# A transformer block on one core: each engine's order of work given as a list, with other bank limits and another start

## The chip, the cores and the metric

The kernel runs on one core of one Trainium2 chip. Five queues of the core appear in the trace: PE (matrix products), ACT, DVE and POOL (work on tiles, element by element), and SP, which here does nothing but start DMA transfers. PEld is PE's loading of the operand that stays in place. The metric is the time of one execution on the device, in microseconds (us). A time is the median of three runs unless the text says otherwise. Where the trace is read, the numbers are those of one profiled execution.

## The reference

One block on x of 2048 rows by 512 columns, float32, with adaptive layer norm, memory-augmented attention (32 heads of 16 columns, four segments of 512 rows) and a feed-forward part of 1792 columns.

```python
mod = (_silu(c) @ w_mod).reshape(c.shape[0], 6, 1, -1)
sa, ca, ga, sb, cb, gb = (mod[:, 0], mod[:, 1], mod[:, 2], mod[:, 3], mod[:, 4], mod[:, 5])
h = _layernorm(x, axis=-1) * (1 + ca) + sa
x = x + ga * _A_ref(h, A_wq, A_wk, A_wv, A_wo, A_beta)
h = _layernorm(x, axis=-1) * (1 + cb) + sb
x = x + gb * _B_ref(h, B_w1, B_b1, B_w2, B_b2)
...
    # inside _A_ref, for each of the four segments s
    logits = jnp.einsum("bhqd,bhkd->bhqk", qs, ks) * scale + mask
    p = _softmax(logits, axis=-1)
    a_dot = jnp.einsum("bhqk,bhkd->bhqd", p, vs)
    num = jnp.einsum("bhld,bhde->bhle", pq, M)
    den = jnp.einsum("bhld,bhd->bhl", pq, z)[..., None] + 1e-6
    o = g * (num / den) + (1.0 - g) * a_dot
    M = M + jnp.einsum("bhld,bhle->bhde", pk, vs)
    z = z + jnp.einsum("bhld->bhd", pk)
...
    # inside _B_ref
    r = jnp.where(h > zero, h, zero)
    out = jnp.einsum("bsf,fd->bsd", r * r, w2) + b2
```

## The kernel before, in words

Most matrix products are made from operands split into a high part and a rest (`hi`, `lo`), three products for one, so every weight and every activation that enters them is first split by a cast on ACT and a subtraction on DVE or POOL.

The attention is cut into 16 units `u` (four segments times four groups of eight heads), each unit into two quads of four heads, 32 quads in all. For a unit, `qk` projects queries and keys (tiles `bqk`, lines L536 to L538), ACT and DVE split them into `sg`, and twelve DMAs on SP spread `sg` into `ST`. For a quad, `a_quad` makes scores only to find each row's maximum (tiles `ba`, L617; ACT copies some to `ac`, DVE reduces the rest at L622). The maxima are transposed on PE (`bat`, L678), negated on ACT (`mt`, L680) and put into a row of `ST` by two small DMAs on SP (L685). `b_quad` then makes the scores again with the maximum inside (`bpb`, L759), ACT takes the exponential into `pt` (L774), POOL clears the masked part, and PE multiplies with the values (`bpv`, L816). ACT copies the result out, PE turns it (`bfin`, L842) and DVE normalises it. `vproj` makes the values (`bv`), `mem` the memory part (`bpkt`, `bmu`, `bmr`). Behind the attention stand the output projection (`bwot`, `bwop`, L900 to L902), the second layer norm (`blnq`, L413, fed by `xh` from DVE, L409) and the feed-forward part (`bh`, `bpf`). At the start, `mod_cols` computes the scale and shift of the first layer norm (`bmod`, L365, then `bmodc`, L385), `split_w` splits wq, wk and wv by four column groups (L476, L479), `ln1` makes `HT`, the transposed input of all projections, and small products of the identity (`bwarm`, L334) fill PE while it has nothing else.

PE runs in three shapes of its array, which the planner calls modes: `F`, the whole array (`bqk`, `bv`, `bwop`, `bh`, `bpf` and the transposes); `R`, two halves of 63 or 64 rows side by side (`ba`, `bpb`); `C`, four groups of 32 columns (`bpv`, `bmod`).

Nothing is left to a scheduler of the language: class `Plan` runs over all steps (`op`), each with an engine, an assumed duration, a due number `pr` and what it needs, and fixes the order of every engine before the program is written. Among the steps that are ready, an engine takes the one with the smallest due number; PE's choice (`pick_pe`) may stay in its mode a little longer (`STAY`), gather an amount (`BATCH`) or wait (`PATIENCE`). PSUM has eight banks, and `POOLS` limits how many each kind may hold: 4 for `#A` (`ba`), 3 for `#B` (`bpb`), 1 for `#V` (`bpv`), 3 for `#D` (most others). Engines keep the order so found, whatever then happens on the chip.

Of the kernel before, what the change touches and what calls it, by code (L numbers as in the profile page):

```python
# [13 lines left out]
ALU = mybir.AluOpType  # L14
# [19 lines left out]

N_WARM = 60
BATCH = {"R": 0, "C": 1.28, "F": 0.28}
K_A = (0.08, 1.18)
K_B = (1.46, 2.6)
K_F = 3.4
K_FF = 3.98  # L40
K_L2 = 0.37
K_LN = (-2.92, -1.85)
# [12 lines left out]
PATIENCE = 1.22  # L55
STAY = {"R": 0.53, "C": 0, "F": 0.38}
# [6 lines left out]
class Plan:  # L63
# [52 lines left out]
    def pick_pe(self, ready):  # L116
        best, amount = {}, {}
        for n in ready:
            if self.can(n):
                if n.mode not in best or (n.pr, n.seq) < (best[n.mode].pr, best[n.mode].seq):  # L120
                    best[n.mode] = n
                amount[n.mode] = amount.get(n.mode, 0.0) + n.dur
        if not best:
            return None
        first = min(best.values(), key=lambda n: (n.pr, n.seq))
        cur = best.get(self.mode)
        if cur is not None and cur.pr <= first.pr + self.stay[self.mode]:
            return cur
        if first.mode == self.mode:
            return first  # L130
        if amount[first.mode] < self.batch[first.mode]:

            rest = [n for m, n in best.items() if m != first.mode and
                    (m == self.mode or amount[m] >= self.batch[m]) and n.pr <= first.pr + self.patience]
            if rest:
                return min(rest, key=lambda n: (n.mode != self.mode, n.pr, n.seq))
        return first

    def run(self):
# [3 lines left out]
        free = dict.fromkeys(engs, 0.0)  # L143
        self.mode = "F"
# [4 lines left out]
        ev, k, t, wire, out = [], 0, 0.0, 0.0, []  # L149
        todo = len(self.nodes)  # L150
        while todo:
            moved = True
            while moved:
                moved = False
                for e in engs:
                    if free[e] > t:
                        continue
                    if e == "PE":
                        n = self.pick_pe(ready[e])
                    else:  # L160
                        n = min((x for x in ready[e] if self.can(x)), key=lambda x: (x.pr, x.seq), default=None)
# [5 lines left out]
                    if e == "PE" and n.mode != self.mode:  # L167
                        s = max(t, free[e] + 0.1) + self.LDW[n.mode]
# [4 lines left out]
                    end = s + n.dur  # L173
                    if n.nb:
# [32 lines left out]
def block_kernel(ctx, tc, x, wq, wk, wv, wo, beta, w1, b1, w2, b2, c, wmod, out):  # L207
# [96 lines left out]
    nc.scalar.dma_start(cs, c[0].rearrange("(k p) -> p k", p=P))  # L304
# [19 lines left out]
    n1 = op("NIL", 4.2, lambda: None, PR0)  # L324
    n1 = op("ACT", 0.2, lambda: nc.scalar.activation(cneg, cs, AF.Exp, scale=-1.0), PR0, after=[n1])
# [818 lines left out]
```

## Time and profile before

| what | value |
|---|---|
| time, median of 3 runs | 841.67 us (841.42 to 841.98) |
| time of the profiled execution | 843.69 us |
| its span, first to last instruction | 842.0 us |
| mean granted clock of TensorE | 0.990 |
| busy time of POOL | 211.5 us (25%) |

The times outside the table stand in the prediction, with their rows. A row of the stretches gives the stretch in us from the span's start, its length, the busy time of each engine with its number of instructions, the granted clock (1.00 is full), the share of time in which the 16 DMA engines moved data, and GB/s. A row of the timeline gives the start, how long it took, engine, line, operation, output and inputs, shape and count, and in brackets the idle time ahead of it with what ended it. Products on PE overlap, so the distance from one start to the next says what a product costs, and its duration does not.

### The profile page before, as it was taken

The page shows a single profiled execution, that of the slowest core. Times are in us where ns is not written, and L with a number is a line of the kernel's source. Part 1 is how long each engine was busy: PE and PEld are TensorE (multiplying, and loading weights), DVE is VectorE, ACT ScalarE, POOL GpSimd, SP SyncE. Part 2 cuts the span into 40 slices and gives each one's busy share as a digit, 9 for nine tenths or more (in the row PEclk, how much of TensorE's full clock was granted, in tenths as well). Part 3 has the DMA queues.
Part 4 walks back from the last instruction along what each step waited for, and adds up shares of the span by engine and source line. Part 5 has one row for each costly group of instructions (what it writes and reads, how often), then busy time and mean ns, then how long its engine had stood idle before and what let it go on. Part 6 is the DMA issues. An engine that isn't in the chain of part 4 may idle for free.

```text
span 842.0 us, 14276 instructions
## 1 busy us (share of the span) xinstructions
PE 819.5 (97%) x4956; PEld 592.8 (70%) x4956; DVE 549.6 (65%) x1503; ACT 441.0 (52%) x907; POOL 211.5 (25%) x262
## 2 busy tenths in 40 slices
PE   9899999999999999999999979999999999999998
PEld 8675666766656666666556657888888888888886
DVE  4678877887887888578879768977534334323223
ACT  2637965678856789567764444454333223322211
POOL 2614542456635666334412110000000000000000
PEclk9899999999999999999999998999999999999999
DMA  8634454232432234322252304233100010001001
GB/s 293 167 90 105 126 172 131 72 77 72 111 77 68 71 76 117 77 66 66 65 150 98 97 18 141 85 100 88 63 1 1 0 51 1 1 0 51 1 0 51
DMA packets 50377, 65.19 MB, mean 77 GB/s; under 512 B 8449, under 2 KB 22529, under 8 KB 50306
## 3 DMA queue, kind: packets, MB, share of 16 engines
q1 hardware_dynamic: 49634, 64.14, 27.2%
q8 instruction: 40, 0.66, 0.3%
q14 instruction: 31, 0.25, 0.1%
q10 hardware_dynamic: 672, 0.13, 0.1%
HBM read 29.91 MB, written 7.34 MB: 44 GB/s over the span
## 4 chain that ended last, share of the span: by engine, by line
PE 85%; DVE 7%; ACT 4%; DMA 2%; issue 1%; SPq 0%; DVEq 0%; ACTq 0%
PE bpv L816 8%; PE bpb L759 7%; PE bh L1065 6%; PE bh L1064 6%; PE bh L1066 6%; PE bpf L1092 6%; PE bpf L1094 6%; PE bpf L1093 6%; PE ba L617 5%; PE bqk L536 4%; PE bqk L537 3%; PE bqk L538 3%; PE bwop L900 2%; PE bv L588 2%; DVE ba L622 2%; PE bwop L902 2%
## 5 line engine op out<-in xcount | busy, mean ns | idle before, releaser
L622 DVE CUSTOM_DVE_ANT_0 ba<-ba,msk 128x512 f32<-128x512 f32 (+2 forms) x384 | 191.8, 533 | 38.2 <-PE ba L617 33.3
L774 ACT ACTIVATE pt<-bpb 128x512 f32<-128x512 f32 x320 | 176.9, 617 | 51.2 <-PE bpb L759 49.2
L1074 ACT ACTIVATE r<-bh,b1c 128x512 f32<-128x512 f32 x56 | 38.5, 688 | 180.4 <-PE bh L1066 163.3
L763 POOL TENSOR_SCALAR_AFFINE_SELECT pt<-pt 128x512 f32<-128x512 f32 x128 | 81.0, 645 | 182.5 <-ACT pt L774 181.0
L1081 DVE TENSOR_TENSOR r<-r 128x512 f32<-128x512 f32 x56 | 38.7, 691 | 126.8 <-ACT rr L1078 126.7
L759 PE MATMUL bpb<-ST 64*128 64x256 f32 (+2 forms) x512 | 87.1, 387 | 1.7 <-DVE X1L L859 1.2
L1092 PE MATMUL bpf<-W,rr 128*128 128x512 f32 x224 | 88.1, 393 | 0.0
L1094 PE MATMUL bpf<-W,rr 128*128 128x512 f32 x224 | 88.0, 393 | 0.0
L1093 PE MATMUL bpf<-W,rr 128*128 128x512 f32 x224 | 88.0, 393 | 0.0
L816 PE MATMUL bpv<-pt,VT 128*32 128x512 f32 (+3 forms) x1024 | 85.2, 443 | 0.9 <-ACT pt L774 0.9
L759 PEld LDWEIGHTS bpb<-ST 64*128 64x128 f32 x512 | 43.3, 184 | 48.4 <-issue 17.0
L617 PE MATMUL ba<-ST 63*128 63x256 f32 (+2 forms) x512 | 72.3, 336 | 1.4 <-ACT lnf L419 0.5
L536 PE MATMUL bqk<-HT,WQK 128*128 128x512 f32 x128 | 58.0, 453 | 3.8 <-ACT HT L426 3.8
L617 PEld LDWEIGHTS ba<-ST 63*128 63x128 f32 x512 | 50.0, 186 | 11.9 <-DVE mx L622 2.2
L816 PEld LDWEIGHTS bpv<-pt,VT 128*32 128x32 f32 x1024 | 26.2, 109 | 41.5 <-issue 35.0
L622 DVE DVE_READ_ACCUMULATOR2_ANT mx<- 128x1 f32 x384 | 54.4, 142 | 0.0
L537 PE MATMUL bqk<-HT,WQK 128*128 128x512 f32 x128 | 51.3, 401 | 0.0
L538 PE MATMUL bqk<-HT,WQK 128*128 128x512 f32 x128 | 51.3, 400 | 0.0
L1092 PEld LDWEIGHTS bpf<-W,rr 128*128 128x128 f32 x224 | 42.1, 188 | 10.0
L1093 PEld LDWEIGHTS bpf<-W,rr 128*128 128x128 f32 x224 | 42.0, 188 | 9.8
L1094 PEld LDWEIGHTS bpf<-W,rr 128*128 128x128 f32 x224 | 42.0, 188 | 9.8
L1064 PE MATMUL bh<-H2a,W 128*128 128x512 f32 x112 | 45.1, 403 | 0.0
(161 smaller groups left out, 1597.4 us busy)
## 6 DMA issues: line engine op xcount, KB each, us to landing
ST<-sg SPq DMA_DIRECT2D x192, 128.0 KB
wr<-in_B_w SPq DMA_DIRECT2D x28, 256.0 KB
xt<-in_A_x SPq DMA_DIRECT2D x16, 256.0 KB
wm<-in_w_mod SPq DMA_DIRECT2D x16, 256.0 KB
xw<-in_A_x SPq DMA_DIRECT2D x16, 256.0 KB
o_dram<-on SPq DMA_DIRECT2D x12, 256.0 KB
ot<-o_dram SPq DMA_DIRECT2D x12, 256.0 KB
out<-X SPq DMA_DIRECT2D x12, 256.0 KB
```

The lines of the kernel that those rows point to most:

```text
L536: nc.tensor.matmul(p, wh, HT[:, 0, k], start=(k == 0), stop=False)
L537: nc.tensor.matmul(p, wh, HT[:, 1, k], start=False, stop=False)
L617: nc.tensor.matmul(dst[:, c0:c0 + n], ST[b:b + 63, 0, sl, qt * P:(qt + 1) * P], ST[b:b + 63, 1, sl, :n], start=True, stop=True)
L622: nc.vector.tensor_tensor_reduce(i, i, msk[:, 512 - n:], scale=1.0, scalar=-3e38, op0=ALU.add, op1=ALU.max, accum_out=o)
L759: nc.tensor.matmul(dst, ST[b:b + 64, 1, sl, kb * P:(kb + 1) * P], ST[b:b + 64, 0, sl, q0:512], start=True, stop=True)
L763: nc.gpsimd.affine_select(out=ap, in_=ap, pattern=[[0, ap.shape[1]], [1, P]], compare_op=ALU.is_ge, fill=0.0, base=0, channel_multiplier=-1)
L774: ns = [act(512, lambda j=j: nc.scalar.activation(buf("P", pt)[:, i + j], bank(keys[j]), AF.Exp, scale=0.25), pr[slot] + 0.01 + 0.001 * j, ...
L816: nc.tensor.matmul(bank(o)[32 * hq:32 * hq + 32, q0:q0 + src.shape[1]], v[:, a:a + 32], src, start=start, stop=stop, tile_position=(0, 32 ...
L1064: nc.tensor.matmul(p, wh, h2[:, 0, k], start=(k == 0), stop=False)
L1092: nc.tensor.matmul(p, rh, FF["W2"][:, f, 0], start=(f == 0), stop=False)
L1093: nc.tensor.matmul(p, rh, FF["W2"][:, f, 1], start=False, stop=False)
L1094: nc.tensor.matmul(p, rl, FF["W2"][:, f, 0], start=False, stop=(f == NF - 1))
```

## The change

The rule by which PE and the other engines chose is gone (`pick_pe`, `STAY`, `BATCH`, `PATIENCE`). In its place stands `ORDER`, a list of step numbers for each of PE, ACT, DVE, POOL and SP, found by a local search over the plan; `Plan.run` hands out steps in the order of the list, and when the next of the list can't start, that engine's turn waits. The assumed durations were set anew, with prices for a change of mode (`TURN`) and for a pause of PE (`PAUSE`, `COLD`).

```diff
-N_WARM = 60
-BATCH = {"R": 0, "C": 1.28, "F": 0.28}
...
+N_WARM = 70
+BANKS = {"#A": 6, "#B": 6, "#V": 1, "#D": 3}
...
-PATIENCE = 1.22
-STAY = {"R": 0.53, "C": 0, "F": 0.38}
+ORDER = {
+    "PE": """
+8 34 61 36 21 37 41 16 12 70 29 39 26 31 74 13 17 75 50 69 30 19 72 59 28 3 15 65 53 32 51 60 40 54 11 83 88 85 90
...
-    LDW = {"R": 0.11, "C": 0.03, "F": 0.11}
+    PAUSE, COLD = 1.3, 5.0
+    TURN = {"RF": 0.19, "FR": 0.17, "RC": 0.09, "CR": 0.09, "CF": 0.19, "FC": 0.15}
...
-                    if e == "PE":
-                        n = self.pick_pe(ready[e])
+                    given = self.given.get(e, ())
+                    if turn[e] < len(given):
+                        n = self.nodes[given[turn[e]]]
+                        n = n if n in ready[e] and self.can(n) else None
+                        turn[e] += n is not None
...
-    nc.scalar.dma_start(cs, c[0].rearrange("(k p) -> p k", p=P))
+    cc2 = sb.tile([KD, 2, P], F32, name="crow", tag="e0")
+    crow, cneg = cc2[:, 0], cc2[:, 1]
+    PL.held["crow"] = [("e", PL.pools["e"].pop(0))]
+    nc.scalar.dma_start(crow, c[0].rearrange("(k p) -> k p", p=P))
...
+    n1 = pe("F", 0.11, lambda: nc.tensor.transpose(bank(("cs",))[:, :KD], crow, ident[:KD, :KD]), PR0 - 1, after=[n1],
+            get=[("#D", ("cs",))], put=["crow"])
+    n_cs = op("ACT", 0.1, lambda: nc.scalar.copy(cs, bank(("cs",))[:, :KD]), PR0 - 1, after=[n1], put=[("cs",)])
...
-            h = act(512, lambda hi=hi, c0=c0: nc.scalar.copy(hi, raw()[:, :, c0]), p, sbuf=True, after=[n], put=put)
+            h = act(512, lambda hi=hi, c0=c0: nc.scalar.copy(hi, raw()[:, :, c0]), p, sbuf=True, after=[n, *(HTN[0] if cc else [])], put=put)
```

The last two pieces are the start: the vector c now comes in as four rows and is turned by PE, and the splits of all but the first column group of wq, wk and wv wait until `HT` of the first segment is done (`HTN[0]`). Ten more `bwarm` products were added. The work itself is the same.

First place, PE from the start of the program to the first projection. Before (`bwarm` are the fillers, `bmod` and `bmodc` the two modulations, `blnq` the transposes of the first layer norm):

```order
L334 MATMUL bwarm<-ident 128x128 x44
L365 MATMUL bmod<-wmod,cs 32x512 x4
L413 MATMUL blnq<-ident,xt 128x128 x8
L385 MATMUL bmodc<-selc,t 128x1 x4
L413 MATMUL blnq<-ident,xt 128x128 x8
L365 MATMUL bmod<-wmod,cs 32x512 x4
L334 MATMUL bwarm<-ident 128x128 x4
L385 MATMUL bmodc<-selc,t 128x1 x4
L334 MATMUL bwarm<-ident 128x128 x12
L536 MATMUL bqk<-HT,WQK 128x512
```

The same stretch of PE now, with the turning of c as `bcs`:

```order
L490 MATMUL bwarm<-ident 128x128 x25
L480 MATMUL bcs<-ident,crow 128x4
L490 MATMUL bwarm<-ident 128x128 x9
L521 MATMUL bmod<-wmod,cs 32x512 x8
L541 MATMUL bmodc<-selc,t 128x1 x8
L569 MATMUL blnq<-ident,xt 128x128 x8
L490 MATMUL bwarm<-ident 128x128 x2
L569 MATMUL blnq<-ident,xt 128x128 x4
L490 MATMUL bwarm<-ident 128x128 x2
L569 MATMUL blnq<-ident,xt 128x128 x4
L490 MATMUL bwarm<-ident 128x128 x19
L694 MATMUL bqk<-HT,WQK 128x512
```

Both modulations now stand together behind 34 fillers; before, the first stood behind 44, and the second behind these, sixteen transposes and the first `bmodc`. Now 57 fillers stand ahead of the first projection (60 before), and the other 13 stand among the first projections.

On ACT the same stretch held, before, from the copies of the two modulations on:

```order
L369 COPY t<-bmod 128x512 x2
L476 CAST WQK<-X1L 128x4x128 x4
L419 ACTIVATE lnf<-blnq,modc 128x128 x2
L426 CAST HT<-lnf 128x4x128
L419 ACTIVATE lnf<-blnq,modc 128x128 x2
```

and now

```order
L525 COPY t<-bmod 128x512 x2
L656 CAST WQK<-X1L 128x4x128
L575 ACTIVATE lnf<-blnq,modc 128x128 x4
L582 CAST HT<-lnf 128x4x128 x2
L575 ACTIVATE lnf<-blnq,modc 128x128 x4
```

Three of the four casts of wq have moved behind the making of `HT`, and with them their subtractions on POOL.

Second place, PE in the middle of the attention. Before, at 128 to 132 us of the span:

```order
L759 MATMUL bpb<-ST 128x512 x2
L816 MATMUL bpv<-pt,VT_106 32x256 x4
L365 MATMUL bmod<-wm,cs 32x512 x4
L759 MATMUL bpb<-ST 128x256 x2
L759 MATMUL bpb<-ST 128x384 x2
L617 MATMUL ba_1650<-ST 128x512
L617 MATMUL ba_1651<-ST 128x512
L617 MATMUL ba_1657<-ST 128x256
L617 MATMUL ba_1657<-ST 128x384
L617 MATMUL ba_1658<-ST 128x256
L617 MATMUL ba_1658<-ST 128x384
L842 MATMUL bfin<-ident,oraw 128x128 x4
```

and now, around the same values (`VT_106`):

```order
L984 MATMUL bpv<-pt,VT_106 32x384 x4
L984 MATMUL bpv<-pt,VT_106 32x128 x4
L984 MATMUL bpv<-pt,VT_106 32x256 x4
L775 MATMUL ba_1792<-ST 128x256
L775 MATMUL ba_1792<-ST 128x384
L775 MATMUL ba_1793<-ST 128x256
L775 MATMUL ba_1793<-ST 128x384
L925 MATMUL bpb<-ST 128x256 x2
L925 MATMUL bpb<-ST 128x384 x2
L925 MATMUL bpb<-ST 128x256 x2
L925 MATMUL bpb<-ST 128x384 x2
L1012 MATMUL bfin<-ident,oraw 128x128 x4
```

The pieces of `bpv` of a quad stand together more often, and so do `ba` and `bpb`. Counted over the whole of PE's order, neighbours of different modes go from 355 to 242: R to F from 103 to 68, F to R from 100 to 60, C to R from 66 to 55, C to F from 10 to 2, R to C from 63 to 47, F to C from 13 to 10.

Third place, PE at the end of the attention. Before (`blnq` is now the second layer norm's transpose, of the first segment):

```order
L816 MATMUL bpv<-pt,VT_107 32x256 x4
L413 MATMUL blnq<-ident,xh 128x128 x4
L842 MATMUL bfin<-ident,oraw 128x128 x4
L413 MATMUL blnq<-ident,xh 128x128 x8
L925 MATMUL bwot<-ident,X1L 128x128 x8
L900 MATMUL bwop<-WVO,oT 128x512
```

and now

```order
L569 MATMUL blnq<-ident,xh 128x128 x4
L984 MATMUL bpv<-pt,VT_107 32x512 x4
L984 MATMUL bpv<-pt,VT_107 32x384 x4
L984 MATMUL bpv<-pt,VT_107 32x128 x4
L984 MATMUL bpv<-pt,VT_107 32x256 x4
L1012 MATMUL bfin<-ident,oraw 128x128 x4
L1097 MATMUL bwot<-ident,X1L 128x128 x12
L1070 MATMUL bwop<-WVO,oT 128x512
```

The last transposes of the second layer norm have moved from behind the last `bpv` to ahead of it, so `bwot`, the turning of the last segment's attention result, now follows the last `bfin` at once. Behind these rows the products `bwop` of the last row tiles stand mixed with one another, and then with the first `bh`.

More of the change, by code (lines that the diff above doesn't have):

```diff
@@ L59, with numbers @@
+2095 2097 1812 2101-2102 2100 2105 2104 1832 2103 2002 1760 2218 2217 2221 2220 2222 2219 2022 2223 2228 2227 2226
[4 rows of a table added]
+""",
+}
+def numbers(text):
+    for word in text.split():
+        a, _, b = word.partition("-")
+        yield from range(int(a), int(b or a) + 1)
 class Node:
@@ L75, in __init__ @@
         self.held = {}
-        self.stay = stay
-        self.batch = batch
-        self.patience = patience
+        self.given = {e: list(numbers(text)) for e, text in order.items()}
     def op(self, eng, dur, fn, pr, after=(), mode=None, get=(), put=(), nb=0):
@@ L114, in drop @@
                     self.pools[pool].append(i)
[L116 to L137, printed above, removed]
     def run(self):
@@ L142, in run @@
         ready = {e: [] for e in engs}
-        free = dict.fromkeys(engs, 0.0)
-        self.mode = "F"
+        free = {"PE": 2.0, "ACT": 2.6, "DVE": 2.7, "POOL": 6.0, "SP": 0.8, "NIL": 0.0}
+        self.mode, turn = "F", dict.fromkeys(engs, 0)
         self.switches = 0
@@ L148, in run @@
                 ready[n.eng].append(n)
-        ev, k, t, wire, out = [], 0, 0.0, 0.0, []
-        todo = len(self.nodes)
+        ev, k, t, wire, out = [], 0, 0.0, 2.6, []
+        for e in engs:
+            k -= 1
+            heapq.heappush(ev, (free[e], k, None, 0))
+        k, todo, idle, cold = 0, len(self.nodes), 0.0, 0.0
         while todo:
@@ L167, in run @@
                     if e == "PE" and n.mode != self.mode:
-                        s = max(t, free[e] + 0.1) + self.LDW[n.mode]
+                        s = t + self.TURN[self.mode + n.mode]
                         self.mode = n.mode
@@ L173, in run @@
                     end = s + n.dur
+                    if e == "PE":
+                        if s - idle > self.PAUSE:
+                            cold = s + self.COLD
+                        end += max(0.0, min(n.dur, (cold - s) / 2))
+                        idle = end
                     if n.nb:
@@ L184, in run @@
             if not ev:
-                raise RuntimeError("stuck: " + str([(n.eng, n.pr, n.get) for e in engs for n in ready[e]][:12]))
+                raise RuntimeError("the plan is stuck")
             t = ev[0][0]
@@ L647, in a_quad @@
         ac = ("ac", u, qd)
-        first = pe("R", 0.34, lambda: m1([bank(k) for k in keys]), pr[0], after=[d for pp in (2 * qd, 2 * qd + 1) for d in STN[u][pp]],
+        first = pe("R", 0.24, lambda: m1([bank(k) for k in keys]), pr[0], after=[d for pp in (2 * qd, 2 * qd + 1) for d in STN[u][pp]],
                    get=[("#A", k) for k in keys] + [("mx", mx), ("ac", ac)])
@@ L835, in b_quad @@
                    put=[("pt", u, qd, n)])
+            if n == 0:
+                turns("V", k)
         VUSE[u].append(k)
@@ L863, in b_quad @@
             if s > 0:
-                k = op("DVE" if last else "POOL", 0.6 if last else 1.45,
+                k = op("DVE" if last else "POOL", 0.6 if last else 1.24,
                        lambda: (nc.vector if last else nc.gpsimd).tensor_tensor(onv(), onv(), TL["am", u], op=ALU.add),
@@ L904, in block_kernel @@
     X1N = {}
-    WOL = []
+    WOL, XWN = [], []
     FF = {}
@@ L945, in ln2 @@
     def ln2(s, pr, wait=()):
-        r = op("DVE", 2.2, lambda: ln_rstd(st_all[:, 4 * s:4 * s + 4], 4), pr[0] - 0.1, after=[X1N[4 * s + t] for t in range(4)])
+        r = op("DVE", 2.2, lambda: ln_rstd(st_all[:, 4 * s:4 * s + 4], 4), pr[0] - 0.1, after=[X1N[4 * s + t] for t in range(4)] + (XWN if s else []))
         H2N[s] = []
```

327 lines of the change are left out of this document (241 added, 86 removed), and 4 rows, old and new, of the table ORDER.

## The prediction

> **What bounds the kernel now.** I read the page first, for its shares of busy time and its chain.
>
> ```profile
> PE 819.5 (97%) x4956; PEld 592.8 (70%) x4956; DVE 549.6 (65%) x1503; ACT 441.0 (52%) x907; POOL 211.5 (25%) x262
> ...
> PE 85%; DVE 7%; ACT 4%; DMA 2%; issue 1%; SPq 0%; DVEq 0%; ACTq 0%
> ```
>
> PE is busy for 97% of the span, and 85% of the chain that ended last is PE's own. So the time can only fall where PE idles, where its clock is low, or where its busy time holds less than it could. Second I read the stretches, cut where the program's stages change.
>
> ```profile
> 0.00:23.20 23.20, 21.22 (x168) 19.09 (x168) 11.35 (x38) 6.45 (x13) 8.04 (x20) 1.00 0.90 283
> 23.20:27.00 3.80, 0.03 (x1) 0.00 (x0) 3.37 (x5) 3.71 (x10) 0.98 (x1) 0.88 1.04 194
> 27.00:33.00 6.00, 5.97 (x14) 4.41 (x15) 3.42 (x6) 4.52 (x10) 3.97 (x4) 0.51 0.82 277
> 33.00:60.00 27.00, 27.00 (x133) 20.53 (x132) 17.78 (x54) 9.91 (x30) 10.46 (x9) 1.00 0.36 85
> 60.00:420.00 360.00, 356.09 (x2673) 228.66 (x2672) 286.47 (x940) 263.15 (x580) 173.13 (x208) 1.00 0.35 91
> 420.00:433.00 13.00, 10.22 (x67) 5.92 (x66) 11.33 (x36) 9.38 (x18) 3.12 (x5) 0.87 0.71 204
> 433.00:496.00 63.00, 62.48 (x421) 41.98 (x420) 48.11 (x132) 30.02 (x60) 11.83 (x18) 1.00 0.25 80
> 496.00:511.00 15.00, 9.43 (x48) 6.91 (x48) 13.18 (x38) 7.87 (x16) 0.00 (x0) 0.77 0.33 104
> 511.00:838.00 327.00, 327.00 (x1440) 265.26 (x1439) 153.67 (x257) 106.00 (x175) 0.00 (x0) 1.00 0.11 33
> 838.00:842.00 4.00, 0.10 (x1) 0.00 (x0) 0.89 (x3) 0.00 (x0) 0.00 (x0) 0.98 0.64 228
> ```
>
> The first busy column is PE's. Three places lose time openly: the start (3.8 us idle, then 6 us at a clock of 0.51), 420 to 433 us (2.8 us idle, clock 0.87) and 496 to 511 us (5.6 us idle, clock 0.77). From 60 to 420 PE idles 3.9 us of 360, and from 511 to 838 not at all; the last 4 us are the final addition and store, which nothing in the change touches. In the feed-forward stretch PE has one mode and one kind of product, so no order can shorten it. What is left is PE's busy time from 33 to 496, and there I read the timeline for what a change of mode costs.
>
> ```profile
> 118.63 0.50 PE L536 MATMUL bqk<-HT,WQK 128*128 128x512 f32 x1
> 118.96 0.39 PE L537 MATMUL bqk<-HT,WQK 128*128 128x512 f32 x1
> 119.19 0.39 PE L538 MATMUL bqk<-HT,WQK 128*128 128x512 f32 x1
> ...
> 120.22 1.06 PE L816 MATMUL bpv<-pt,VT 128*32 128x512 f32 x8
> 121.10 1.04 PE L365 MATMUL bmod<-wm,cs 128*32 128x512 f32 x8
> 122.07 0.50 PE L759 MATMUL bpb<-ST 64*128 64x256 f32 x4
> 122.41 0.39 PE L617 MATMUL ba<-ST 63*128 63x512 f32 x2
> 122.73 0.50 PE L536 MATMUL bqk<-HT,WQK 128*128 128x512 f32 x1
> ...
> 414.78 0.39 PE L537 MATMUL bqk<-HT,WQK 128*128 128x512 f32 x1
> 415.00 0.39 PE L538 MATMUL bqk<-HT,WQK 128*128 128x512 f32 x1
> 415.32 0.50 PE L759 MATMUL bpb<-ST 64*128 64x256 f32 x4
> ```
>
> A `bqk` among its like takes 0.22 to 0.23 us from start to start (118.96 to 119.19, 414.78 to 415.00). The last one ahead of a change takes 0.32 (415.00 to 415.32), and the first one behind a change takes 0.33 (118.63 to 118.96). So a change costs 0.10 on the way out and 0.10 on the way in. It is the same for the others: `ba`, half the array at 512 columns, takes 0.32 ahead of `bqk` (122.41 to 122.73); the four `bpb` of 256 columns, two passes of half a `bqk`, take 0.34 instead of 0.23 behind a change (122.07 to 122.41); `bmod` takes 0.97 ahead of `bpb`, where the like `bpv` ahead of it in the same mode took 0.88. That `bpv` itself had just come in from `bqk`, so the way into C is nearly free. None of this shows as idle time; 355 changes at up to 0.20 are some 65 us inside PE's busy 819.5.
>
> **The change part by part.** *The order of PE.* The counts stand above: 94 changes fewer into F or R, at 0.20 each 18.8 us, and 19 fewer into C, at 0.10 each 1.9 us. Not every kind of group shows its way in here, so I take 20 of these 20.7 us. The bounds are 11 (113 changes, the way out alone) and 23 (113 at 0.20). All of it is on the path, since PE idles so little between 60 and 420.
>
> *The start.*
>
> ```profile
> 1.98 11.81 PE L334 MATMUL bwarm<-ident 128*128 128x128 f32 x88 [1.98 <-POOL ident masks.py:199]
> ...
> 17.48 1.06 PE L365 MATMUL bmod<-wmod,cs 128*32 128x512 f32 x8
> ...
> 19.23 2.18 ACT L476 CAST WQK<-X1L 128x512 fp32r<-128x512 f32 x4
> ...
> 20.45 3.73 POOL L479 TENSOR_TENSOR WQK<-X1L,WQK 128x512 fp32r<-128x512 f32 x3 [14.46 <-DMA ST<-pad]
> ...
> 27.03 0.79 PE L536 MATMUL bqk<-HT,WQK 128*128 128x512 f32 x1 [3.81 <-ACT HT L426]
> ```
>
> A filler is two records, so one takes 11.81 / 44 = 0.27 us. The second `bmod` starts at 17.48, and from there it is 9.55 us to the first projection, through ACT, which had four casts of wq in that way; three move behind, 1.6 us. Both `bmod` now stand behind 34 fillers, 9.1 us after 1.98. Their weights are the second and third MB that SP fetches, and at the 283 GB/s of the first stretch these 3.1 MB are there at 11 to 12 us. So `HT` could be ready at 12 + 8 = 20. But PE's own queue ahead of the projection, 57 fillers (15.3) and the `bmod`, `bmodc` and `blnq` after 1.98 (21.22 busy in the first stretch less 60 fillers is 5.1), lasts to 22.4; I take 23. That is 4.0 earlier, and with no pause ahead of it the clock stays full, where 27 to 33 lost 2.9. Of these 6.9 the 13 fillers among the projections take back 3.5. I take 3, with 0 and 7 as bounds (7 if all 13 fall into waits). The moved splits are covered by those fillers and the first 24 projections, 5.5 us: POOL takes 1.25 us for each of six, and if it is late, the projections of unit 1 wait about that long. The turning of c (one product, one copy) lies under the 34 fillers, and DVE's three short steps for it now go ahead of the layer norm's statistics. The added `bcs` costs nothing while the fillers last.
>
> *420 to 433 us.*
>
> ```profile
> 423.77 1.06 PE L816 MATMUL bpv<-pt,VT 128*32 128x512 f32 x8 [0.65 <-ACT pt L774]
> ...
> 426.57 0.51 PE L759 MATMUL bpb<-ST 64*128 64x256 f32 x4 [1.25 <-DVE X1L L859]
> ```
>
> Here output projections, modulation of the last segment and attention meet, and DVE is busy 11.33 of 13. The list sets other work between. At stake are 2.8 us of idle time and up to 0.13 x 13 = 1.7 us of clock; I take 3, with bounds 0 and 4.5. The clock fell at these pauses, the longest 1.25 us. [...]
>
> *The end of the attention.*
>
> ```profile
> 500.51 0.66 PE L842 MATMUL bfin<-ident,oraw 128*128 128x128 f32 x4
> 502.97 0.63 PE L413 MATMUL blnq<-ident,xh 128*128 128x128 f32 x4 [1.80 <-DVE xh L409]
> 506.32 1.12 PE L413 MATMUL blnq<-ident,xh 128*128 128x128 f32 x4 [2.72 <-DVE xh L409]
> ...
> 502.74 0.25 DVE L856 RECIPROCAL dn<-bfin 128x16 f32<-128x16 f32 x1
> ...
> 505.12 0.68 DVE L865 TENSOR_TENSOR X1L<-X1L,am 128x512 f32<-128x512 f32 x1
> ```
>
> The `blnq` that waited 4.5 us for DVE now stand ahead of the last `bpv`. With the lower clock (0.23 of the 9.43 us busy: 2.2) 7.8 us are at stake. But the `bwot` that follow the last `bfin` at once need that quad normalised and added: 0.9 us from L856 through L859 and 0.68 for L865, so about 2 us with the handovers, and ahead of `bfin` the copy on ACT, about 1 more. This chain was hidden behind the waiting `blnq`; it is what is late next. Another us goes to the splits ahead of `bwop`. I take 7.8 - 4 = 4, with bounds 0 and 8.
>
> *The wait that each list adds.* An engine whose next step isn't ready now holds everything behind it; on PE that is all products. The order of before was as fixed, and idled 3.9 us in 360. The new one packs the same DVE work (286.47 us there) into some 17 us less, 84% instead of 80%, so pauses must grow. Below zero the term can't go by more than those 3.9. Above, 0.65 us, the wait of the `bpv` at 423.77, once in each of the 32 quads (one `mt` each, L680 below) is 21. I take 5, that is 9 us of idle time instead of 3.9, nearer to the row of 360 us than to that of 13. The other limits of banks cost nothing by themselves: there are eight as before.
>
> The sum against the span of 842.0: -20 - 3 - 3 - 4 + 5 = -25, so 817.0. Around the span lie 843.69 - 842.0 = 1.7 us, and the profiled execution is 2.0 above the median of the runs; the forecast for the median is 817.0 + 1.7 - 2.0 = **816.7 us**.
>
> **The rivals.** *Emptying becomes the bound* (15%). PE saves its changes and waits for ACT and DVE instead, at the 21 us of the upper bound: 816.7 + 16 = 833 at worst, 828 in the middle. For it speaks 420 to 433, where DVE at 87% went with 2.8 us of pauses in 13; against it 433 to 496, with 0.5 us in 63 at 76%. [...]
>
> *The clock* (5%). If pauses like that at 426.57 come in eight more places, each can bring the 1.7 us of clock of that stretch on top of the idle time already counted: 8 x 1.7 = 13.6, so 830.
>
> *SP's queue, slower* (5%).
>
> ```profile
> L680 ACT ACTIVATE mt<-bat x32: 248/261/284, 59.1 to 470.7; 16x128 fp32r<-16x128 f32 x32
> ...
> 126.59 8.59 SPq L566 DMA_DIRECT2D ST<-sg  x12
> 135.27 1.42 SPq L685 DMA_DIRECT2D ST<-mt  x2
> ...
> 144.94 0.50 PE L759 MATMUL bpb<-ST 64*128 64x512 f32 x2
> ```
>
> The row of maxima (`mt`) of one quad waited here behind twelve transfers of `sg`, issued over 8.59 us, and went out at 135.27. Nobody noticed, since the first `bpb` of that quad came at 144.94. The new order brings `bpb` closer behind `bat`. If in each of the 16 units one row came later than PE's place for it by more than 25 / 16 = 1.6 us, the gain would be gone; at 3 us, a third of the wait above, it is 816.7 + 48 = 865. Against it: the new SP order cuts about half of these sixteen dozens in two, with an `mt` between.
>
> *The change does nothing* (3%): the changes of mode would have to lie beside other waits; 3.9 us of idle time in 360 leaves no room for that.
>
> **How the numbers follow.** The forecast has 72%, from 804 (waits at their lower bound, the start at 7) to 826; the rivals have 15, 5, 5 and 3%. The range 804 to 832 leaves out the last two, the tail of the first two and some 4% below, 18% together. A measurement of this kernel tells about 0.2% from no change, 1.7 us. Faster by more: 72 + 15 + 5 = 92%; within: 3%; slower: 5%.
>
> **What would show it.** The first `bqk` at about 23 us with no stretch of 0.5 clock behind it; `bfin` of the last quad some 25 us before 500.5; stretches of 60 to 420 in which PE idles about 9 us in 340; a `bwot` that waits about 2 us for DVE L865's like; the feed-forward stretch at 327 us again. I am wrong if PE idles over 20 us between 60 and 470, if `bpb` waits for SP's transfers of `mt`, or if a change of mode turns out cheaper than 0.20 where runs are longer.

## The result, and the profile after

The changed kernel takes **815.11 us** (median of 4 runs, 813.78 to 816.33), the kernel before on the same chip 841.54 (841.02 to 841.98): a ratio of 0.9686, with a 95% interval of 0.9669 to 0.9703, so 26.4 us or 3.1% less. The forecast was 816.7, its range 804 to 832.

The page of the changed kernel, its shares of busy time and its chain:

```profile
PE 796.9 (98%) x4977; PEld 591.8 (73%) x4977; DVE 556.3 (68%) x1503; ACT 442.2 (54%) x908; POOL 211.4 (26%) x262
...
PE 86%; DVE 9%; ACT 2%; issue 1%; DMA 1%; SPq 0%; POOL 0%; DVEq 0%; ACTq 0%; POOLq 0%
```

PE has 21 records more than before (ten fillers of two records each, and the turning of c) in 22.6 us less busy time. No product was taken away, so its busy time held something that is gone. The stretches, cut again where the stages change (columns as in the prediction; the granted clock is the third figure from the end):

```profile
0.00:23.33 23.33, 21.35 (x164) 19.66 (x164) 16.41 (x43) 9.12 (x20) 5.30 (x17) 1.00 0.90 285
23.33:37.00 13.67, 13.67 (x75) 11.52 (x74) 10.34 (x18) 8.23 (x17) 12.80 (x10) 1.00 0.84 225
37.00:60.00 23.00, 21.02 (x102) 15.65 (x101) 17.17 (x51) 9.48 (x30) 5.38 (x6) 1.00 0.44 117
60.00:410.00 350.00, 344.57 (x2700) 231.53 (x2700) 292.53 (x937) 265.99 (x580) 174.04 (x208) 1.00 0.38 101
410.00:461.00 51.00, 50.99 (x372) 35.23 (x372) 47.05 (x143) 30.07 (x63) 10.03 (x16) 1.00 0.23 76
461.00:486.00 25.00, 21.72 (x153) 16.03 (x150) 18.08 (x46) 13.17 (x26) 3.84 (x6) 0.93 0.30 92
486.00:809.40 323.40, 323.40 (x1424) 262.19 (x1423) 153.84 (x269) 106.14 (x176) 0.00 (x0) 1.00 0.10 32
```

The first projection comes at 23.33 us instead of 27.03, and the clock behind it stays full (1.00 from 23.33 to 60 us). Where before had 2.8 us of pauses and a clock of 0.87 (420 to 433), PE now rests 0.01 us in 51. PE idles 5.4 us of 350 in the long stretch, where before it was 3.9 of 360. The feed-forward stretch has no pause (323.40 us busy of 323.40), as before. Two places still lose time openly. From 37 to 60 us PE idles 2.0 us of 23, where before it idled not at all from 33 to 60. The other is the end of the attention, as its timeline shows:

```profile
472.48 2.36 PE L984 MATMUL bpv<-pt,VT 128*32 128x512 f32 x32
476.11 0.66 PE L1012 MATMUL bfin<-ident,oraw 128*128 128x128 f32 x4 [1.27 <-ACT oraw L1008]
476.60 0.49 PE L1097 MATMUL bwot<-ident,X1L 128*128 128x128 f32 x3
478.51 2.00 PE L1097 MATMUL bwot<-ident,X1L 128*128 128x128 f32 x9 [1.42 <-DVE X1L L1035]
...
480.74 0.63 PE L1071 MATMUL bwop<-WVO,oT 128*128 128x512 f32 x1
481.17 0.63 PE L1072 MATMUL bwop<-WVO,oT 128*128 128x512 f32 x1
```

The last `bfin` stands 24.4 us ahead of where it stood (500.51), and waits for ACT's copy. The `bwot` behind it waits for DVE. Behind these two pauses `bwop` goes from start to start in 0.43 us (480.74 to 481.17), where a `bwop` at 468.92 took 0.23. The granted clock is 0.52 over the 3.50 us from 478.60 to 482.10; outside of it no stretch read in this execution is below 0.98.

### The profile page after: what moved, and what is told of

It reads as the page before. It is cut to its first block, busy times and chain, and to the rows that moved or that the text cites. A ratio compares the mean times of both kernels' runs of the same rounds, so it can differ in the third digit from the quotient of the medians.

```text
span 813.4 us, 14336 instructions
## 1 busy us (share of the span) xinstructions
PE 796.9 (98%) x4977; PEld 591.8 (73%) x4977; DVE 556.3 (68%) x1503; ACT 442.2 (54%) x908; POOL 211.4 (26%) x262
## 4 chain that ended last, share of the span: by engine, by line
PE 86%; DVE 9%; ACT 2%; issue 1%; DMA 1%; SPq 0%; POOL 0%; DVEq 0%; ACTq 0%; POOLq 0%
PE bpv L984 8%; PE bh L1231 6%; PE bh L1233 6%; PE bh L1232 6%; PE bpf L1259 6%; PE bpf L1260 6%; PE bpf L1261 6%; PE bpb L925 6%; PE ba L775 6%; PE bqk L694 3%; PE bqk L695 3%; PE bqk L696 3%; DVE ba L780 2%; PE bwarm L490 2%; PE bfin L1012 2%; PE bwop L1070 2%
## 5 line engine op out<-in xcount | busy, mean ns | idle before, releaser
L780 DVE CUSTOM_DVE_ANT_0 ba<-ba,msk 128x384 f32<-128x384 f32 (+2 forms) x384 | 192.1, 531 | 24.7 <-PE ba L775 13.7
L942 ACT ACTIVATE pt<-bpb 128x512 f32<-128x512 f32 x320 | 169.7, 617 | 14.5 <-PE bpb L925 11.0
L984 PE MATMUL bpv<-pt,VT 128*32 128x512 f32 (+3 forms) x1024 | 80.5, 438 | 0.0
L925 PE MATMUL bpb<-ST 64*128 64x256 f32 (+2 forms) x512 | 71.9, 352 | 0.9 <-DVE mx L780 0.9
L775 PEld LDWEIGHTS ba<-ST 63*128 63x128 f32 x512 | 44.5, 185 | 31.0 <-ACT pt L942 6.8
L925 PEld LDWEIGHTS bpb<-ST 64*128 64x128 f32 x512 | 45.6, 185 | 29.3 <-issue 8.2
L1245 ACT ACTIVATE rr<-r 128x512 fp32r<-128x512 f32 x56 | 35.4, 632 | 39.8 <-PE bpf L1261 38.6
L694 PE MATMUL bqk<-HT,WQK 128*128 128x512 f32 x128 | 55.7, 435 | 0.0
L717 POOL TENSOR_SCALAR e<-e 128x512 f32<-128x512 f32 x24 | 35.7, 1488 | 61.7 <-ACT e L713 61.5
L696 PE MATMUL bqk<-HT,WQK 128*128 128x512 f32 x128 | 50.4, 394 | 0.0
L695 PE MATMUL bqk<-HT,WQK 128*128 128x512 f32 x128 | 50.3, 393 | 0.0
```

The source lines that it names most:

```text
L694: nc.tensor.matmul(p, wh, HT[:, 0, k], start=(k == 0), stop=False)
L695: nc.tensor.matmul(p, wh, HT[:, 1, k], start=False, stop=False)
L696: nc.tensor.matmul(p, wl, HT[:, 0, k], start=False, stop=(k == KD - 1))
L775: nc.tensor.matmul(dst[:, c0:c0 + n], ST[b:b + 63, 0, sl, qt * P:(qt + 1) * P], ST[b:b + 63, 1, sl, :n], start=True, stop=True)
L780: nc.vector.tensor_tensor_reduce(i, i, msk[:, 512 - n:], scale=1.0, scalar=-3e38, op0=ALU.add, op1=ALU.max, accum_out=o)
L925: nc.tensor.matmul(dst, ST[b:b + 64, 1, sl, kb * P:(kb + 1) * P], ST[b:b + 64, 0, sl, q0:512], start=True, stop=True)
```

## The experiments

Each ratio is to runs of the kernel before on the same chip, whose median was 842.5 to 843.5; the changed kernel's own 0.9686 was taken beside the lower 841.54. Against the changed kernel, a difference is (ratio - 0.9686) x 842. Its uncertainty comes from both intervals and is some 2 us; two kernels that were measured side by side compare better. Some differences are given a second way: the profiled execution of the experiment is matched with that of the changed kernel, product by product, and the text says how far PE is ahead or behind at a time. That shows where time goes, but for one execution of each.

**The price of a change of mode, by itself.** In the feed-forward stretch PE has one mode and no pauses (323.40 us busy of 323.40 in the changed kernel). One small step was put there behind each of the 56 `bh`, in three shapes. Its output is read by nobody.

```diff
+    def extra(s):
+        def mm():
+            h2 = LT["H2"][s % 2]
+            nc.tensor.matmul(bank(("dum",)), h2[:, 0, 0, 0:P], h2[:, 0, 0, :], start=True, stop=True)
+        return mm
```

That is e5_F. In e5_R the product has 63 rows, in e5_C it is four products of 32 columns:

```diff
-            nc.tensor.matmul(bank(("dum",)), h2[:, 0, 0, 0:P], h2[:, 0, 0, :], start=True, stop=True)
+            nc.tensor.matmul(bank(("dum",)), h2[0:63, 0, 0, 0:P], h2[0:63, 0, 0, :], start=True, stop=True)
```

e5_F: 

> The changed kernel with 56 more products in the feed-forward stretch, one behind each bh, on the whole array (128 rows, 512 columns) into a bank of their own that nobody reads: no change of mode. Both theories: 56 x 0.23 = 12.9 us more than 815.1, so 828.0.

e5_R: 

> The same 56 products at the same places, but on 63 rows (half the array), so with 112 changes of mode, half of them out of and half into the whole-array mode. Theory (0.10 out and 0.10 in for each): 112 x 0.20 = 22.4 us more than the kernel with 56 whole-array products, so 850.4. Rival (changes are cheap or lie beside other work): within 3 us of 828.0.

e5_C: 

> At the same 56 places four products on 128 rows and 32 columns of the array each (128 columns of data, ordinary floating point), that is a quarter of a bpv; 112 changes, into and out of the mode of columns. Alone the four take about a quarter of the 0.88 us of a bpv, 0.22. Theory (0.10 out of the whole array, 0.02 into the columns, 0.10 out of them, 0.10 into the whole array): 56 x (0.22 + 0.32) = 30 us more than 815.1, so 845. Rival (cheap): 828.

Measured: e5_F 829.35 us, ratio 0.9843 (0.9827 to 0.9860), 13.2 more than the changed kernel; e5_R 850.22, 1.0087 (1.0072 to 1.0102); e5_C 846.22, 1.0042 (1.0028 to 1.0056), 30.0 more than the changed kernel. The timeline around one such step (`bdum`), of e5_R and then of e5_C:

```profile
561.15 0.40 PE L1236 MATMUL bh<-H2a,W 128*128 128x512 f32 x1
561.47 0.50 PE L1291 MATMUL bdum<-H2a 63*128 63x512 f32 x1
561.90 0.50 PE L1262 MATMUL bpf<-W,rr 128*128 128x512 f32 x1
562.24 0.40 PE L1263 MATMUL bpf<-W,rr 128*128 128x512 f32 x1
```

```profile
561.88 0.40 PE L1236 MATMUL bh<-H2a,W 128*128 128x512 f32 x1
562.21 0.42 PE L1293 MATMUL bdum<-H2a 128*32 128x128 f32 x8
562.57 0.50 PE L1262 MATMUL bpf<-W,rr 128*128 128x512 f32 x1
562.90 0.40 PE L1263 MATMUL bpf<-W,rr 128*128 128x512 f32 x1
```

In e5_F every start there follows the last by 0.22 to 0.24 us. With the half array the three steps are 0.32, 0.43 and 0.34, so 0.09 on the way out of the whole array, 0.20 for the step that comes in and goes out, and 0.11 on the way back in. Over 56 places e5_R takes 20.9 us more than e5_F, **0.186 us for each of 112 changes**; expected was 0.20. The rival (cheap changes) is out by a factor of seven. With columns it is 0.33, 0.36 and 0.33, and 30.0 us against 30 expected. The step's 0.36, less an estimated 0.22 for its products (a quarter of the 0.88 of a `bpv`), leaves 0.14 for its way in and its way out. With the 0.09 that `bmod` took more on its way out in the kernel before (0.97 against 0.88), some 0.05 are left for the way into the columns, an estimate.

**The same changes put back into the attention.** First, at 26 places a whole-array step was moved ahead of the last half-array step of a run (one of them, in the list of PE: 942 and 939 are `ba`, 853 is a `bpb`, 1170 a step of `bqk`):

```
-942 853 939 1170 978 1171
+942 853 1170 939 978 1171
```

e8_split: 

> The changed kernel, but at 26 places of the attention one whole-array step is moved ahead of the last half-array step of a run, which puts 52 changes of mode back (294 instead of 242) and adds no product. Theory (each change costs 0.20 us of PE's time wherever it stands): 52 x 0.20 = 10.4 us more than the changed kernel's 815.1, so 825.5, give or take 2 for waits. Rival (the changes are cheap, and the gain came from the order of the waits): at most 2 us more, 815 to 817.

Measured: 817.40 us, 0.9700 (0.9678 to 0.9723), so 1.2 us more than the changed kernel, where 10.4 were expected. The price at the place is right, as the timelines of the changed kernel and then of e8_split show at this place:

```profile
173.82 0.39 PE L925 MATMUL bpb<-ST 64*128 64x512 f32 x2
174.06 0.39 PE L775 MATMUL ba<-ST 63*128 63x512 f32 x2
174.38 0.50 PE L694 MATMUL bqk<-HT,WQK 128*128 128x512 f32 x1
...
175.18 0.60 PE L885 MATMUL bpkt<-ident,phi 128*128 128x128 f32 x4
175.53 0.48 PE L694 MATMUL bqk<-HT,WQK 128*128 128x512 f32 x1
```

```profile
172.26 0.41 PE L925 MATMUL bpb<-ST 64*128 64x512 f32 x2
172.60 0.50 PE L694 MATMUL bqk<-HT,WQK 128*128 128x512 f32 x1
...
173.49 0.50 PE L775 MATMUL ba<-ST 63*128 63x512 f32 x2
173.92 0.66 PE L885 MATMUL bpkt<-ident,phi 128*128 128x128 f32 x4
174.33 0.48 PE L694 MATMUL bqk<-HT,WQK 128*128 128x512 f32 x1
```

The same steps take 2.07 us instead of 1.71, 0.36 for two changes. So it is at 16 of the 26 places (0.29 to 0.40 each). At the other ten it is under 0.25, since the step that was moved filled a wait there. Over all 26 that makes 6.8 us, by matching each step of PE in both traces. But at the end of the attention PE is only 2.8 us later: the other 4.0 came back between the places, at waits for other engines, which got shorter. One of them in the changed kernel:

```profile
224.92 0.56 PE L925 MATMUL bpb<-ST 64*128 64x256 f32 x3 [0.74 <-DVE mx L780]
```

In e8_split the same `bpb` has no listed wait. Another 1.5 us came back at 476 to 482 us: 0.3 from a shorter wait of `bfin` (0.96 instead of 1.27), the rest from the clock, which did not fall there in this execution (1.00 from 474 to 486 us, against 0.86 in the changed kernel). So the forecast for this run failed, and not by the price: PE that is late at one place waits less at the next.

The 26 places were those where a step could be moved without waiting for its inputs, and some filled a wait. A second pair avoids that choice. Ahead of 56 half-array steps, spread evenly over those that stand behind another one, stands a product of 16 columns, on 63 rows in one kernel and on all 128 in the other; nothing is moved.

```diff
+    def ahead(n, step):
+        def go():
+            nc.tensor.matmul(bank(n.get[0][1])[:, 0:16], ident, ident[:, 0:16], start=True, stop=True)
+            step()
+        return go
```

That is e10_whole; e10_half has `ident[0:63]` and `ident[0:63, 0:16]`.

e10_half: 

> The changed kernel with 56 very small products (16 columns, ordinary floating point, on 63 rows like the scores) in the attention, each ahead of a half-array step that stands behind another one; they write where the step behind them writes next. No change of mode is added: 242. Each should take less than the 0.27 us of a filler of 128 columns: between 2 and 15 us more than 815.1.

e10_whole: 

> The same 56 small products at the same places on all 128 rows: 112 more changes of mode, 354, which is the count of the kernel before (355) in the order of the changed one. Against e10_half: theory 1 (every change is 0.19 us on the path) 21 us more. Theory 2 (0.19 at the place, but PE's waits behind it shrink, as where 52 changes were put back; there are some 8 us of such waits between 60 and 461 us, and then they are used up) 13 us more. Rival (waits take the same share as there, 7 of 10) 6 us more.

Measured: e10_half 819.39 us, 0.9720 (0.9706 to 0.9733); e10_whole 832.60, 0.9875 (0.9862 to 0.9889). The difference is 0.0155 +- 0.0019, **13.1 us (11.4 to 14.7) for 112 changes, 0.117 each**. That is theory 2's 13, though not quite in its way. Matched step by step, the two profiled executions differ by 17.1 us around the 56 places themselves, not by 21. Behind the first small product the two half products start 0.13 us apart in e10_half, and 0.01 in e10_whole; that e10_half pays the other 4 us there is an estimate. From 60 to 480 us the difference between the two executions grows by 11.9. So 5.2 of 17.1 us came back, spread evenly over that time. By that share 21.0 us of changes are worth 14.6; with 13.1 as the lower end, **13 to 15 us**. The stretch from 60 to 461 us, of the changed kernel and then of e10_whole:

```profile
60.00:461.00 401.00, 395.56 (x3071) 266.76 (x3070) 339.59 (x1079) 296.06 (x642) 184.08 (x224) 1.00 0.36 98
```

```profile
60.00:461.00 401.00, 398.35 (x3056) 268.24 (x3055) 327.69 (x1044) 287.47 (x618) 181.43 (x219) 1.00 0.35 96
```

PE's idle time there falls from 5.4 to 2.7 us: with the changes back, PE waits less for the others, whose work in the same 401 us has grown thinner (DVE 328 us busy instead of 340). That is only part of what came back; where the rest lies no row shows.

**The start alone.**

e1b_start: 

> The new start alone (c fetched in rows and turned by a product, casts of the later weight columns behind the layer norm, the order of every engine up to the first scores as in the changed kernel, but without the 13 fillers among the projections), with the order of before from there on and the old bank limits; 353 changes of PE's mode instead of 355. Theory (start = a small term): 3 to 7 us under the kernel before, so 834.5 to 838.5, with the first bqk near 23 us instead of 27 and no half clock behind it. Rival (the old order gives it all back before the first bpb, which stood at 63.3 us before and 63.1 after): within 1 us of 841.5.

The kernel that ran under this label is not the one that its expectation describes: it had the new start, but the old rule and the old due numbers, which then planned everything anew (371 changes of mode, and both `bmod` where the rule put them). It took 852.06 us, 1.0106 (1.0092 to 1.0119), with the first `bqk` at 28.51 us after a wait of 3.8 for `HT`. That says how far the old rule throws the order about when its input changes a little, and nothing about the start. A still earlier version with given lists and the old bank limits (e1_start) has no time: its plan got stuck, with no engine able to start its next step. The kernel meant is e1c_start. Outside the start its order of PE is that of before, product by product.

```diff
-BANKS = {"#A": 6, "#B": 6, "#V": 1, "#D": 3}
+BANKS = {"#A": 4, "#B": 3, "#V": 1, "#D": 3}
...
+    OFF = {35, 57, 49, 66, 55, 77, 44, 71, 43, 67, 47, 27, 56}
```

(and in `ORDER` each engine's list is the changed kernel's up to the first scores, then the order of before; the fillers in `OFF` do nothing).

e1c_start: 

> The start alone, with the rest held fixed: up to the first scores every engine's order is that of the changed kernel (without the 13 fillers among the projections, as in e7_nofill), from there on every engine has the order of before written out as a list, and the bank limits are those of before (4 and 3). Theory (the start is worth 3, with 0 and 7 as bounds, and the 13 fillers are not there to take anything back): 3 to 7 us under the kernel before, so 834.5 to 838.5, with the first bqk at about 23 us. Rival (the old order gives it back, since DVE, ACT and the transfers of sg that it waits for do not move): within 1 us of the kernel before.

Measured: 844.72 us (12 runs), 1.0015 (1.0004 to 1.0027), so 1.3 us slower than before. The first `bqk` comes 5.0 us earlier, and then PE's timeline reads:

```profile
22.05 0.48 PE L689 MATMUL bqk<-HT,WQK 128*128 128x512 f32 x1
...
29.62 0.39 PE L691 MATMUL bqk<-HT,WQK 128*128 128x512 f32 x1
32.57 0.80 PE L741 MATMUL bv<-WVO,HT 128*128 128x512 f32 x1 [2.55 <-ACT WVO L651]
37.41 0.79 PE L742 MATMUL bv<-WVO,HT 128*128 128x512 f32 x1 [4.05 <-DVE lny L553]
...
L654 POOL TENSOR_TENSOR WVO<-w,WVO x3: 1257/1257/1713, 33.2 to 36.1; 128x512 fp32r<-128x512 f32 x3
```

The old order goes from the projections straight to `bv`, which needs all of wv split. Those splits now stand behind the layer norm, and POOL's last one, begun at 36.1, takes 1.26 us and ends at 37.4 (the last row gives the shortest, middle and longest duration in ns, and the first and last start; the row of `bv` names a step of DVE that ended at that time too). So PE waits 6.6 us, and behind the second wait `bv` goes from start to start in 0.43 us (38.00 to 38.43; granted clock 0.82 from 33 to 60 us). From 46 to 300 us it is 2.1 us behind the kernel before. The list of the changed kernel has the projections of one more unit and the first `ba` in that place; its first `bv` stands at 43.76. So the new start is worth nothing without the new order behind it.

**The fillers among the projections.** The 13 fillers of `OFF` do nothing; all else is the changed kernel.

e7_nofill: 

> The changed kernel without the 13 fillers that stand among the first projections. Theory (they take PE's time there): 13 x 0.27 = 3.5 us less, so 811.6. Rival (they fill waits for the casts of the next weight columns): 815.1 as before. Third: without them PE pauses, its clock falls to a half for some 3 us, and the time is 816 to 818.

Measured: 812.60 us, 0.9637 (0.9619 to 0.9654), 4.1 us less than the changed kernel, and the fastest of all: its interval lies below that of the changed kernel (0.9669 to 0.9703). The stretches of e7_nofill where they stood:

```profile
20.00:32.00 12.00, 12.00 (x69) 10.32 (x68) 7.98 (x14) 9.18 (x21) 8.08 (x7) 1.00 0.94 231
32.00:38.00 6.00, 4.05 (x14) 3.05 (x13) 5.77 (x10) 2.19 (x5) 5.92 (x5) 0.72 0.76 208
```

Both things that were expected happen: PE saves the fillers' time, and then pauses 1.95 us for POOL with a lower clock behind it (0.72 from 32 to 38 us, and `bqk` 0.57 us from start to start at 35.02). The saving is the larger. The size is less sure than that: in the profiled executions e7_nofill is 1.6 us ahead at 60 us, 2.1 at 450, 3.7 at 490 and 2.3 from 520 on. In two of its four runs the mean granted clock is 1.000, against 0.995 in the other two, so there the clock did not fall, and those runs took as long as the others (812.83 and 812.16 us, against 812.79 and 812.42).

**The end of the attention.** First undone: the last 30 steps of PE in the attention, and what the other engines do for them, in the order of before (2598 and 2604 are the last two `blnq`, 2440 to 2442 the last `bpv`, 2444 the last `bfin`, 2711 the first `bwot`).

```
...
-2541 2419 2578 2579 2598 2580 2581 2604 2440 2441 2442 2444 2711
+2431 2575 2436 2441 2578 2579 2592 2580 2581 2442 2598 2444 2604 2711
```

e9_oldend: 

> The changed kernel, but the last 30 steps of PE in the attention, and what ACT, DVE and POOL do for them, stand in the order of before (the two last blnq around the last bfin again). Theory (the end was worth 4): about 819 instead of 815.1, with pauses of PE before the last blnq and a low clock behind them. Rival (the place of the blnq does not matter, since the wait only moves to bwot): 815 to 816. If everything that was at stake there comes back, 823.

Measured: 822.38 us, 0.9753 (0.9735 to 0.9770), 5.6 us more than the changed kernel. Its timeline:

```profile
482.65 1.09 PE L569 MATMUL blnq<-ident,xh 128*128 128x128 f32 x4 [1.80 <-DVE xh L565]
483.53 0.85 PE L1097 MATMUL bwot<-ident,X1L 128*128 128x128 f32 x3
486.00 2.18 PE L1097 MATMUL bwot<-ident,X1L 128*128 128x128 f32 x9 [1.62 <-DVE X1L L1035]
```

The wait for DVE's `xh` is back, and the one of `bwot` stays: in this order both are paid. Matched with the changed kernel, e9_oldend is 0.1 us behind at 450 us and 7.5 at 490, so all of the loss lies here. Not all of it is the old end's: at the seam PE also waits 1.4 us for POOL's `pt`, which neither the kernel before nor the changed one does there, and eight changes of mode more (250) are some 1.5 us at 0.186 each. The end is then worth **some 5 to 7 us**.

Then mended further: the last `bpv` ahead of the last `blnq` (2604) and of the last step of `bwop` (2581), which now stand on the two sides of `bfin`, and ACT and DVE taking that quad first.

```
-2598 2580 2581 2604 2440 2441 2442 2444 2711
+2598 2580 2440 2441 2442 2604 2444 2581 2711
```

e4_end: 

> The changed kernel with its end of the attention mended: the last bpv one step earlier, one blnq between it and bfin, the last step of bwop between bfin and bwot, ACT copying oraw ahead of the last layer norm's split, and DVE taking the last normalisation ahead of bwop's addition and statistics. Theory (PE's pauses of 1.27 and 1.42 us and the half clock behind them, 1.6 us, are lost time): 1.0 us less for the pauses, and 1.6 more if the clock then stays full: 812.5 to 814.1 instead of 815.1. Rival (what follows waits for something else): 815.

Measured: 813.70 us, 0.9656 (0.9639 to 0.9672), 2.5 us less than the changed kernel, with some 2 us of uncertainty. The waits of PE from 474 to 530 us in e4_end (engine and line, for whom, us in all, times, longest):

```profile
PE bwot L1097 <- DVE X1L L1035: 1.4, 1, 1.4
PE bwop L1072 <- DVE oT L1105: 1.0, 1, 1.0
PE bh L1233 <- DVE W L1200: 0.6, 1, 0.6
```

The pause ahead of `bfin` is gone and the clock stays full (1.00 from 474 to 530 us), but two new waits for DVE stand behind. In the profiled execution they take back nearly all of it: 1.5 us ahead at 490 us, 0.1 from 520 on (spans 813.3 and 813.4).

Last, no fillers and a mended end together, with half of the W1 splits on POOL to relieve DVE. The end is not the one of e4_end: the last `bpv` stay behind the last `blnq`, and ACT's list is that of the changed kernel, although the expectation says that ACT takes that quad first.

```diff
-        W1N[f] = dve(512, lambda: nc.vector.tensor_tensor(FF["W1"][:, f, 1], wv_(), FF["W1"][:, f, 0].bitcast(F32), op=ALU.subtract),
+        e, eng = ("POOL", nc.gpsimd) if f % 2 else ("DVE", nc.vector)
+        W1N[f] = op(e, 1.24 if f % 2 else 0.6, lambda: eng.tensor_tensor(FF["W1"][:, f, 1], wv_(), FF["W1"][:, f, 0].bitcast(F32),
...
-2598 2580 2581 2604 2440 2441 2442 2444 2711
+2598 2580 2604 2440 2441 2442 2444 2581 2711
```

e11_best: 

> The changed kernel with both gains put together: no fillers among the projections; at the end of the attention the last step of bwop behind bfin, and DVE and ACT taking that quad first; and in the feed-forward the lower halves of every second column block of W1 on POOL, which does nothing there, instead of DVE, which is busy for 95 to 98% from 490 to 530 us. Theory (the two gains add, since POOL takes what DVE had no time for): 4.1 and 2.5 us less than 815.1, so 808.5, with no wait for DVE's W between 480 and 530. Rival (the start of the feed-forward waits for the weights all the same and takes back 1 to 2 of it): 810 to 811.

Measured: 814.15 us, 0.9661 (0.9641 to 0.9682), 2.1 us less than the changed kernel, and not better than e7_nofill. Matched step by step with the changed kernel, it is 5.4 us ahead at 510 us, 1.7 at 530 and 1.4 from 546 on. One stretch of it, and what PE waited for there:

```profile
515.00:525.00 10.00, 8.41 (x29) 6.15 (x28) 9.52 (x23) 4.32 (x8) 2.93 (x2) 0.83 0.36 105
```

```profile
PE bpf L1265 <- ACT W L1213: 0.9, 1, 0.9
PE bpf L1266 <- DVE W L1214: 0.6, 1, 0.6
```

The rival is right and too mild: the weights of the feed-forward are not ready for a PE that comes 5 us earlier, and the lower clock of that stretch (0.83) adds to it. The same happened on a smaller scale in e4_end and e7_nofill, which lost 1.4 us of their lead each between 490 and 520 us, with one listed wait of 0.6 us for `W`. So what is gained ahead of the feed-forward is in part taken back at its weights. Moving splits to POOL did not remove these waits; whether its slower subtractions (1.31 us for a split of wq in the changed kernel, against 0.68 for one of W1 on DVE) made them worse was not tried.

## Why the prediction was right, step by step

- **The order of PE, -20.** The count was right and so, nearly, was the price: 113 changes at the 0.186 of e5_R are 21.0 us of PE's time. (One of the prediction's signs of being wrong was a change cheaper than 0.20; it is 7% cheaper.) What did not hold is the sentence that all of it is on the path: by the e10 pair 13 to 15 us are. The other 6 to 8 belong to the term of the waits. An engine that saves 21 us asks the others for the same work in less time.
- **The waits that the lists add, +5.** The sign was right, the size is 6 to 8 by the runs. The sum of the two terms was -15, and measured is -13 to -15. The prediction said that they would show as idle time (9 us in 340), and only 5.4 in 350 do. Where the rest lies no row shows. The other bank limits were put at nothing; no run has the new order with the old limits, so that stays untested.
- **The start, -3.** The first projection came at 23.33, as forecast, and the clock stayed full (1.00 to 60 us). Of these 3.7 us and the clock little is left. At 64 us, just behind the first `bpb`, the changed kernel has done 72 `bqk`, 30 `ba` and 20 `blnq`, the kernel before 70, 28 and 16, and the same of everything else but fillers and `bcs`. That is about 1 us of work by the distances in the timelines, inside the bounds of 0 and 7. The fillers took 2 to 4 us of it (2.3 and 4.1 by the two ways in e7_nofill, 3.5 in the forecast), and the 2.0 us of pauses from 37 to 60 were not in the sum. What the prediction took for granted is that the moved splits are covered by what stands ahead of them. That holds for the new order alone: with the old one, `bv` waits 6.6 us for them and the start brings nothing (e1c_start).
- **420 to 433 us, -3.** In the changed kernel neither pause nor low clock is left there (0.01 us idle in 51, clock 1.00), which would be 4.5. That is read from the trace; no run took this part alone.
- **The end of the attention, -4.** By e9_oldend it is some 5 to 7. The waits that were forecast as new are the ones seen: `bfin` 1.27 for ACT's copy (about 1 was said), `bwot` 1.42 for DVE (about 2).
- **The sum.** 13 to 15, 1, 4.5 and 5 to 7 are 23 to 28, around the 26.4 us measured. That the forecast came within 2 us is in part luck: the start was put some 2 us too high, and the two other places 1 to 3 us too low each.

Of the rivals, *emptying becomes the bound* is partly there in its effect: waits took 6 to 8 of the 21 us, a little more than the 5 of the forecast and far from the 21 of the rival's upper end. Whether PE waited for banks to be emptied, or for what ACT and DVE make from them, no run separates. *The clock* did not come true: one stretch of half clock is left (0.52 over 3.50 us), where before had three (0.50 over 6.83, 3.41 and 6.83 us). *SP's queue* did not either: no `bpb` in the changed kernel has a listed wait for a transfer of `mt`.

## What to carry to other kernels

A change of PE's mode cost 0.186 us here (e5_R against e5_F), which no idle row showed; it was read as the longer distance between two starts (0.32 us instead of 0.23), and a few products put into a stretch that only PE bounds gave its price. That price times the count was the upper end of what fewer changes saved: three to four tenths of it did not reach the time, in part because PE's waits for other engines grew, and gains ahead of the feed-forward were in part lost again at its weights. An order found by search fits together with the start and the end that it was found with: parts of it, taken alone, gained nothing or lost, and a small one (13 fillers) could still be left out for 2 to 4 us.

## What the runs showed of the hardware

In these runs the length of a pause of PE did not tell whether the clock fell behind it. Ahead of `bpkt` PE paused 1.95 us in e7_nofill and 1.96 in e11_best; the two `bqk` behind it stand 0.57 us from start to start in the first and 0.31 in the second:

```profile
34.41 0.95 PE L889 MATMUL bpkt<-ident,phi 128*128 128x128 f32 x4 [1.95 <-POOL phi L722]
35.02 0.78 PE L698 MATMUL bqk<-HT,WQK 128*128 128x512 f32 x1
35.59 0.63 PE L699 MATMUL bqk<-HT,WQK 128*128 128x512 f32 x1
...
33.93 0.66 PE L890 MATMUL bpkt<-ident,phi 128*128 128x128 f32 x4 [1.96 <-POOL phi L723]
34.34 0.48 PE L699 MATMUL bqk<-HT,WQK 128*128 128x512 f32 x1
34.65 0.40 PE L700 MATMUL bqk<-HT,WQK 128*128 128x512 f32 x1
```

The pair of pauses at the end of the attention, 1.27 and 1.42 us in the changed kernel, came again as 1.25 and 1.42 in e10_half, and there the clock stayed full (1.00, against 0.86). The stretch around it, of the changed kernel and then of e10_half:

```profile
474.00:486.00 12.00, 9.31 (x57) 7.46 (x50) 8.23 (x24) 3.59 (x7) 0.00 (x0) 0.86 0.54 172
...
478.00:490.00 12.00, 9.33 (x71) 6.29 (x69) 8.32 (x20) 4.62 (x9) 0.00 (x0) 1.00 0.50 155
```

In the kernel before, the granted clock was 0.50 from 26.08 to 32.91 us, from 428.85 to 432.26 and from 503.95 to 510.78:

```profile
26.08:32.91 6.83, 5.88 (x13) 4.37 (x14) 3.91 (x7) 5.32 (x12) 3.88 (x4) 0.50 0.87 291
428.85:432.26 3.41, 3.41 (x22) 1.63 (x21) 2.69 (x12) 1.96 (x5) 0.14 (x1) 0.50 0.66 213
503.95:510.78 6.83, 4.46 (x16) 3.87 (x17) 6.07 (x21) 3.60 (x8) 0.00 (x0) 0.50 0.71 225
```

The longest pause from 415 us to the second of them was 1.25 us (at 426.57). What decides whether the clock falls, no run shows.

Leaving the whole array took 0.09 us for half of it (e5_R, 0.32 against 0.23) and 0.10 for columns (e5_C, 0.33), and coming back 0.11 and 0.10 (0.34 and 0.33). In e10_half, a product of 16 columns on half the array, ahead of others of its mode, added 2.9 us in 56 places by the ratios, and 5.3 from 60 to 450 us in the profiled execution, so 0.05 to 0.1 each.
